# Moving whole rounds of a short convolution from TensorE to VectorE, in front of a chain of matrix products

## The chip, the cores and the metric

One NeuronCore of a Trainium2 chip runs the kernel. TensorE multiplies matrices into PSUM, VectorE (DVE) and ScalarE (ACT) evict and combine, GpSimd (POOL) casts while it starts DMAs, SyncE (SP) starts the other DMAs and the transposing ones. The metric is the device time of one execution in microseconds (us), the median over runs; before the change it is 519.52 (519.33 to 520.88, three runs).

## The reference

The input x has 8 sequences of 3904 tokens with 192 channels. First comes a causal convolution of 7 taps along the tokens; the taps of each of the 8 heads (24 channels each) are a softmax. Its output goes, token by token, through two products side by side, their elementwise product, and two further products:

```
w   = softmax(weight)                            # 8 heads x 7 taps
out[b, s, c] = sum_k w[head(c), k] * x_padded[b, s + k, c]
a = out @ w1; b = out @ w2                       # 192 -> 1024
h = a * b @ w3                                   # 1024 -> 1024
result = h @ w_out                               # 1024 -> 192
```

The kernel multiplies w3 by w_out once at its start (`w3_product`, into W_sb), so that two products are left per token: the first (192 to 2 x 1024) and the second (1024 to 192).

## The kernel before

**Tokens.** The 31232 tokens are two streams (r = 0, 1) of 15616. A round R is 512 tokens of both streams; there are 31, the last one half as long. `first_product(R)` makes, for each of eight slices ft of 128 columns, the halves pa and pb: six matmuls each of 64 rows x 512 columns (three channel groups, two streams), the two streams on the two halves of the array's rows. ScalarE casts pa to asb (line 464), VectorE multiplies asb by pb into abT (line 466). pa, pb and all other PSUM tiles share four buffers of two banks (`banks`). `second_product(R, r)` multiplies abT by W_sb into ops (line 482), ScalarE copies it to osb (line 487), SP stores it (line 490).

**Phases.** After a start in which rounds 0 to 2 have their first product between all the loading of weights, the loop runs phases p = 0 to 14. Phase 0 has no first product; phase p has those of rounds 2p+1 and 2p+2. Then come the second products of rounds 2p and 2p+1, four in all. Every engine executes its instructions in the order in which the program gives them; nothing reorders them. SP and POOL are such queues too: a DMA that must wait holds back all DMAs that are behind it on its engine. SP's DMAs use eight completion semaphores in turn, so that each also waits for the landing of the one eight places ahead.

**The convolution on TensorE.** Windows of 32 tokens (26 new ones and 6 of overlap) are loaded by POOL into xb and cast to bf16 (`load_x`, line 127). A unit (`conv`) multiplies the windows of one block, for some heads' channels, by 32x32 banded matrices of the taps (line 296, into cps); ScalarE evicts to convo (line 305). When a block is complete, `store` writes it by SP to the DRAM tensor rows (lines 331, 337), and `transposes(R)` reads 512 tokens back with a transposing DMA for each of three groups k of 64 channels (both streams side by side, 128 rows) into the ring xT, which has place for four rounds (line 371). The first product reads xT. Blocks 0 to 3 have 20, 20, 20 and 40 windows and all 192 channels; blocks 4 to 11 have 64 (the last 56) and only the first 128 channels. Units of 48 and of 64 matmuls alternate; the table `places` puts one or two of them into a phase, behind its first and its third second product.

**The convolution on VectorE.** From round 5 on, the last 64 channels (k = 2) are VectorE's. `cast_c` copies two rounds of x by POOL to the DRAM tensor rows_c in bf16 (line 396), `raw_transpose` brings them by one transposing DMA of 1040 columns to the tile raw (line 402), and `conv_c` applies the seven taps with a multiplication and multiply-adds over 1024 columns (lines 412, 416), the last of them into xT[2]. The taps come as a column per channel, wC: SP stores the softmax to DRAM and reads it back spread over the partitions (`load_taps`, lines 379, 385). The call of `conv_c` in phase p stands between the first products and the second products, for the rounds of phase p+1; the raw transpose for the next phase is issued at a phase's end, ahead of the xT transposes.

**Loads.** From phase 1 on, POOL issues one block of x a phase, after a tiny copy (`pace`) that waits for the last multiply of the phase's first round.

## Time and profile before

| what | value |
|---|---|
| median of three runs | 519.52 us |
| the profiled execution's own time | 521.78 us |
| its span, first to last instruction | 519.8 us |
| TensorE busy | 512.5 us, 99% |
| VectorE busy | 423.0 us, 81% |
| ScalarE busy | 339.0 us, 65% |
| POOL busy | 82.3 us, 16% |
| mean granted clock of TensorE | 0.997 |
| first product, one matmul of 64x512 | 373 ns, two at a time |
| multiply into abT | 1221 ns, 240 of them |

The chain of work that ended last is 96% TensorE's. A group's idle time is the time of its engine just before it, with what ended most of it. In the chain in order of time and in the timeline, the first number is the start in us from the span's start, the second the length. In the table of windows the columns are the length, then each engine's busy time with its number of instructions (PE, PEld, DVE, ACT, POOL), the granted clock of TensorE, the busy share of the DMA engines and GB/s. SPq marks SP's issuing of DMAs.

### The profile page before, as it was taken

Reading aid. Unit: us, or ns where it says so; the run is one execution under the profiler, and the core shown is the slowest. Engines: PE = TensorE matmul, PEld = TensorE weight load, DVE = VectorE, ACT = ScalarE, POOL = GpSimd, SP = SyncE. Lnnn points to the kernel's source line nnn. Section 1 sums busy time; section 2 is a strip of 40 time slices with the busy share of each in tenths; the row PEclk is TensorE's granted clock in tenths of the full one; section 3 lists DMA queues with packets and bytes.
Section 4 is the critical chain, followed back from the end, with each engine's and each line's share of the span. In section 5 each row is a group of like instructions: output and inputs, shape, how many; then the busy total and the mean of one; then the engine's idle time right before and its main releaser. Section 6 shows DMA issues by size and latency. Waiting matters only on the chain.

```text
span 519.8 us, 14514 instructions
## 1 busy us (share of the span) xinstructions
PE 512.5 (99%) x6276; PEld 337.7 (65%) x6276; DVE 423.0 (81%) x408; ACT 339.0 (65%) x368; POOL 82.3 (16%) x143
## 2 busy tenths in 40 slices
PE   8999999899999999999999999999999999999997
PEld 4446846647658475584755858558485584856777
DVE  6898187599797996979979799797997979979670
ACT  6886586476675757757566575767757657476562
POOL 8866003023030220302700000000000000000000
PEclk9999999899999999999999999999999999999999
DMA  9999979969597697955991422905615076240304
GB/s 139 152 182 147 151 167 148 189 123 126 154 95 144 135 127 156 144 129 82 176 214 32 132 53 58 183 12 128 122 60 126 1 181 62 63 106 3 122 1 153
DMA packets 164270, 60.76 MB, mean 117 GB/s; under 512 B 113139, under 2 KB 164207, under 8 KB 164207
## 3 DMA queue, kind: packets, MB, share of 16 engines
q1 hardware_dynamic: 92719, 42.65, 36.7%
q0 software_dynamic: 71472, 17.19, 36.2%
q8 instruction: 49, 0.80, 0.6%
q14 instruction: 14, 0.11, 0.1%
q10 hardware_dynamic: 16, 0.00, 0.0%
HBM read 34.66 MB, written 34.82 MB: 134 GB/s over the span
## 4 chain that ended last, share of the span: by engine, by line
PE 96%; ACT 1%; DMA 1%; issue 1%; DVE 1%; POOL 0%; DVEq 0%; POOLq 0%
PE ops L482 32%; PE pa L457 30%; PE pb L457 30%; PE cps L296 2%; PE wps L547 1%; DMA xb<-in_x_dram 1%; ACT asb L464 1%; DVE abT L466 0%; ACT convo L305 0%; PE ops L500 0%; PE tps L361 0%; PE tps L346 0%; POOL xb L127 0%; DVE xT L353 0%; PE warm L206 0%
## 5 line engine op out<-in xcount | busy, mean ns | idle before, releaser
L466 DVE TENSOR_TENSOR abT<-asb,pb 128x1024 bf16<-128x1024 bf16 x240 | 292.9, 1221 | 72.5 <-ACT asb L464 56.8
L464 ACT CAST asb<-pa 128x1024 bf16<-128x1024 f32 x244 | 247.0, 1012 | 63.4 <-PE pa L457 63.1
L457 PE MATMUL pb<-xT,wn 64*128 64x512 bf16 (+1 forms) x744 | 198.3, 373 | 0.0
L457 PE MATMUL pa<-xT,wn 64*128 64x512 bf16 (+1 forms) x744 | 197.5, 373 | 0.2
L457 PE MATMUL pa<-xT,ws 64*128 64x512 bf16 (+1 forms) x744 | 197.5, 373 | 0.0
L457 PE MATMUL pb<-xT,ws 64*128 64x512 bf16 (+1 forms) x744 | 196.2, 373 | 0.0
L457 PEld LDWEIGHTS <-wn 64*128 64x128 bf16 x1488 | 138.2, 94 | 86.0 <-issue 2.2
L457 PEld LDWEIGHTS <-ws 64*128 64x128 bf16 x1488 | 131.8, 94 | 70.8 <-POOL ws L192 0.4
L482 PE MATMUL ops<-W_sb,abT 128*128 128x192 bf16 x1936 | 166.8, 247 | 0.0
L482 PEld LDWEIGHTS <-abT 128*128 128x128 bf16 x1936 | 159.6, 98 | 7.2 <-issue 6.2
L487 ACT COPY osb<-ops 128x768 f32<-128x768 f32 (+1 forms) x61 | 48.4, 794 | 102.9 <-PE ops L482 102.9
L416 DVE SCALAR_TENSOR_TENSOR acc<-raw,wC,acc 128x1024 f32<-128x1024 bf16 (+8 forms) x80 | 83.0, 1066 | 1.9
L305 ACT CAST convo<-cps 128x1024 bf16<-128x1024 f32 (+3 forms) x46 | 37.7, 876 | 3.9 <-PE cps L296 3.8
L127 POOL DMA_DIRECT2D xb<-in_x_dram x54 | 38.0, 713 | 2.8 <-PE pa L457 1.6
L638 POOL COPY pace<-abT 1x2 bf16<-1x2 bf16 x6 | 1.0, 174 | 161.3 <-DVE abT L466 161.3
L396 POOL DMA_DIRECT2D rows_c<-in_x_dram x26 | 19.8, 766 | 3.5 <-issue 2.4
L416 DVE SCALAR_TENSOR_TENSOR xT<-raw,wC,acc 128x512 bf16<-128x512 bf16 (+1 forms) x26 | 18.1, 739 | 0.4
L296 PE MATMUL cps<-xb,Aband 32*32 32x192 bf16 (+6 forms) x1216 | 14.6, 225 | 2.5 <-issue 2.0
L296 PEld LDWEIGHTS <-Aband 32*32 32x32 bf16 x1216 | 10.6, 88 | 8.2 <-issue 7.0
L412 DVE TENSOR_SCALAR acc<-raw,wC 128x1024 f32<-128x1024 bf16 (+1 forms) x13 | 9.7, 749 | 2.1 <-DMA raw<-rows_c 2.1
L504 DVE COPY osb<-ops 128x192 f32<-128x192 f32 x1 | 0.4, 358 | 11.7 <-PE ops L500 11.7
L528 POOL DMA_DIRECT2D w3b<-in_moe_w_dram x12 | 7.1, 598 | 4.0 <-DMA xb<-in_x_dram 3.4
(63 smaller groups left out, 75.0 us busy)
## 6 DMA issues: line engine op xcount, KB each, us to landing
out_dram<-osb SPq DMA_DIRECT2D x60, 384.0 KB
xb<-in_x_dram POOLq DMA_DIRECT2D x16, 256.0 KB, 7.0
rows<-convo SPq DMA_DIRECT2D x25, 128.0 KB
rows_c<-in_x_dram POOLq DMA_DIRECT2D x22, 128.0 KB, 5.8
rows<-convo SPq DMA_DIRECT2D x25, 80.0 KB
xb<-in_x_dram POOLq DMA_DIRECT2D x8, 240.0 KB, 6.8
xb<-in_x_dram POOLq DMA_DIRECT2D x6, 216.0 KB, 5.5
w3b<-in_moe_w_dram POOLq DMA_DIRECT2D x4, 256.0 KB, 5.0
```

What stands on the lines that cost most here:

```text
L127: nc.gpsimd.dma_start(out=xb[group(r, e), s:s + w, :], in_=bass.AP(tensor=x.tensor, offset=(r * TS + t - PAD) * D, ap=[[D, C], [E * ST * D ...
L296: nc.tensor.matmul(o.rearrange("p (w g) -> p w g", g=wd)[:, :, c - c0:c1 - c0], Aband[group(r, e), h, :], xb[group(r, e), s:s + m, c:c1], ...
L305: f(out=convo[:, e::E, k, :, lo:lo + c] .rearrange("p w r g -> p r w g"), in_=src[:, :, :, o:o + c])
L396: nc.gpsimd.dma_start(out=rows_c[t0:t1, r * Q:r * Q + Q], in_=x_rows[r * TS + t0:r * TS + t1, WC:D])
L412: nc.vector.tensor_scalar(out=out, in0=raw[:, HALO + lo - t0 - d:HALO + hi - t0 - d], scalar1=wC[:, K - 1 - d:K - d], scalar2=None, op0=AL ...
L416: nc.vector.scalar_tensor_tensor(out=out, in0=raw[:, HALO + lo - t0 - d:HALO + hi - t0 - d], scalar=wC[:, K - 1 - d:K - d], in1=acc[:, lo ...
L457: nc.tensor.matmul(p[:, r, f * N:f * N + N], w_of(i, k, r)[rs, ft * 128:(ft + 1) * 128], xT[k][rs, r0:r0 + N], start=(k == 0), stop=(k == ...
L464: nc.scalar.copy(out=asb[:, :, 0:per * N], in_=pa[:, :, 0:per * N])
L466: nc.vector.tensor_tensor(out=ab[:, f0, :, 0:N], in0=asb[:, :, 0:N], in1=pb[:, :, 0:N], op=ALU.mult)
L482: nc.tensor.matmul(ops[:, g // 2, (g % 2) * D:(g % 2) * D + D], ab[:, jt, r, g * 128:(g + 1) * 128], W_sb[:, jt, :], start=(jt == 0), stop ...
L487: nc.scalar.copy(out=osb.rearrange("p (a g) d -> p a (g d)", g=2), in_=ops[:, 0:ng // 2, 0:2 * D])
L528: nc.gpsimd.dma_start(out=t[C * i:C * i + C], in_=bass.AP(tensor=moe_w3.tensor, offset=j0 * 128 * DFF + i * GQ, ap=[[DFF, C], [C * DFF, 4 ...
```

## The change

The four phases 4, 7, 10 and 13 (SIDE) get the convolution of both their rounds, all three channel groups, from VectorE; all other rounds get it from TensorE.

- `side_cast`, `side_transpose` and `side_conv` take the place of `cast_c`, `raw_transpose` and `conv_c`: one channel group k of one SIDE phase at a time. Phases 1, 2, 3 convolve k = 0, 1, 2 for phase 4, phases 4, 5, 6 for phase 7, and so on to phase 12. The result is the tile side, which the first product reads in place of xT (`operand`). Input, accumulator and result live in buffers that the loading of w3 used. The raw transpose is two DMAs (528 and 512 columns).
- TensorE's blocks have all 192 channels: sizes 40, 40, 80, 80, 80 and 32 after block 3. Blocks 6, 7 and 8 (80 windows) feed the four rounds between two SIDE phases. Units have two heads (32 matmuls, 240 columns) in the blocks of 80 and four heads (64 matmuls) in the others. Block 6 is stored in phase 3, block 7 in phase 6, block 8 in phase 9, and their twelve transposes are issued at that phase's end, for the phase after next.
- At a phase's end the xT transposes are issued first and the raw ones behind them.
- `load_taps` moves from the loads of round 0's first product to the end of round 2's, behind the transposes of rounds 3 and 4; it fills 64 partitions for all three groups with ten DMAs, and POOL copies them to the other 64 at the start of phase 1.
- Loads of x and casts are lists of single DMAs (`x_jobs`), of which some are issued after each of five slices of a phase's first products, each time behind a `pace` copy.
- In phase 0 the two units stand behind the first and the second of the second products, and VectorE evicts half of each.
- The outputs of the last two rounds are stored in halves, and the last two copies change engines.

```diff
-    SIZES = [20, 20, 20, 40] + [64] * 7 + [56]
-    SPLIT = 4
+    SIDE = (4, 7, 10, 13)
+    SIZES = [20, 20, 20, 40, 40, 40, 80, 80, 80, 32]
...
+    def side_transpose(p, k):
+        t0, t1 = side_span(p)
+        raw_of[p, k] = stage.tile([128, HALO + 2 * CH], BF16, tag="w3T", bufs=2, name="raw")
+        for lo, hi in ((t0 - HALO, t0 + CH), (t0 + CH, t1)):
+            nc.sync.dma_start_transpose(
+                out=raw_of[p, k][:, HALO + lo - t0:HALO + hi - t0], in_=rows_c[lo:hi, k, :])
+
+    def side_conv(p, k):
+        t0, t1 = side_span(p)
+        if p not in side_of:
+            side_of[p] = stage.tile([128, NP, 2 * CH], BF16, tag="w3b0", bufs=1, name="side")
+        raw = raw_of.pop((p, k))
+        acc = stage.tile([128, 2 * CH], FP32, tag="w3b4", bufs=1, name="acc")
...
+        for d in range(2, K):
+            for lo, hi in zip([t0] + [z + d for z in starts], starts + [t1]):
+                add(acc[:, lo - t0:hi - t0], lo, hi, d)
+        add(side_of[p][:, k, :], t0, t1, 0)
+
+    def operand(R, k, rs):
+        if phase_of(R) in SIDE:
+            t0 = R * CH - side_span(phase_of(R))[0]
+            return side_of[phase_of(R)][rs, k, t0:t0 + width(R)]
+        a = ring_of[R] * CH % RING
+        return xT[k][rs, a:a + width(R)]
...
-        load_taps()
-        cast_c(0)
+        for f in side_cast(SIDE[0], 0):
+            f()
         load_x(5)
...
-               (store, 3), (transposes, 3), (transposes, 4))})
+               (store, 3), (transposes, 3), (transposes, 4), (load_taps,))})
...
-    places = {0: 2, 1: 2, 2: 1, 3: 1, 4: 2, 5: 1, 6: 1, 7: 1, 8: 1, 9: 2, 10: 1, 11: 1}
+    places = {0: (0, 1), 1: (0, 2), 2: (0, 2), 3: (0, 2), 4: (0,), 5: (0,), 6: (0, 2), 7: (0,),
+              8: (0,), 9: (0, 2), 10: (0,), 11: (0,)}
+    tasks = {q - NP + k: (q, k) for q in SIDE for k in range(NP)}
+    jobs = {p: side_cast(*tasks[p + 1]) for p in range(1, len(phases)) if p + 1 in tasks}
+    for p, b, part in ((1, 6, 0), (1, 6, 1), (2, 7, 0), (3, 7, 1), (5, 8, 0), (6, 8, 1), (8, 9, 0)):
+        jobs[p] = jobs.get(p, []) + x_jobs(b, part)
+    points = ((0, 1), (0, 4), (0, 7), (1, 2), (1, 5))
...
+        if p == 1:
+            P(out=wC[Q:128], in_=wC[0:Q])
...
-        if 0 < p <= len(chunks):
-            conv_c(p - 1)
+        if p in tasks:
+            side_conv(*tasks[p])
...
-        if p < len(chunks):
-            raw_transpose(p)
-        while sent[0] < NR and sent[0] <= LAG + 2 * p + 4 and \
-                min((sent[0] + 1) * CH, TS) <= stored[0]:
-            transposes(sent[0])
-            sent[0] += 1
+        while due:
+            transposes(due.pop(0))
+        if p + 1 in tasks:
+            side_transpose(*tasks[p + 1])
```

More of the change, by code (lines that the diff above doesn't have):

```diff
@@ L46, with phase_of, windows @@
     ST = C - PAD
-    WB = -(-S // ST)
-    NWIN = (B // NS) * WB
-    LAST = S - (WB - 1) * ST
     LAG_ROWS = (LAG + 1) * CH
-    SIZES = [20, 20, 20, 40] + [64] * 7 + [56]
-    SPLIT = 4
-    WC = 2 * Q
-    assert sum(SIZES) == NWIN
+    SIDE = (4, 7, 10, 13)
+    SIZES = [20, 20, 20, 40, 40, 40, 80, 80, 80, 32]
     NB = len(SIZES)
     FIRST = [sum(SIZES[:b]) for b in range(NB)]
-    RC = FIRST[SPLIT] * ST // CH
-    XN = 32 * WC
+    XN = 20 * D
     HW = 6
+    def phase_of(R):
+        return (R - 1) // 2
+    def windows(t0, t1):
+        out = []
+        while t0 < t1:
+            n = min(ST, t1 - t0, S - t0 % S)
+            a = min(t0, TS - ST)
+            out.append((a, t0 - a, t0 - a + n))
+            t0 += n
+        return out
+    conv_rounds = [R for R in range(NR) if phase_of(R) not in SIDE]
+    ring_of = {R: i for i, R in enumerate(conv_rounds)}
+    t0 = (LAG + 3) * CH
+    spans = [(0, t0), (t0, t0 + SIZES[4] * ST), (t0 + SIZES[4] * ST, (2 * SIDE[0] + 1) * CH)]
+    for q, nxt in zip(SIDE, SIDE[1:] + (NR,)):
+        spans.append(((2 * q + 3) * CH, min((2 * nxt + 1) * CH, TS)))
+    wins = []
+    for i, (t0, t1) in enumerate(spans):
+        ws = windows(t0, t1)
+        size = sum(SIZES[:4]) if i == 0 else SIZES[3 + i]
+        assert len(ws) <= size
+        wins += ws + [(ws[-1][0], 0, 0)] * (size - len(ws))
+    assert len(wins) == sum(SIZES)
     def tok(i):
-        return (i // WB) * S + (i % WB) * ST
+        return wins[i][0]
     const = ctx.enter_context(tc.tile_pool(name="const", bufs=1))
@@ L80 @@
     rows = dram.tile([TS, NP * NS * Q], BF16, name="rows")
-    rows_c = dram.tile([TS, NS * Q], BF16, name="rows_c")
+    rows_c = dram.tile([TS, NP, NS * Q], BF16, name="rows_c")
     taps_d = dram.tile([H, K], FP32, name="taps_d")
@@ L89, in shape_of @@
         return n, m, n // m
-    def width_of(b):
-        return D if b < SPLIT else WC
     def parts_of(b):
-        return [range(4)] if 4 * shape_of(b)[1] * width_of(b) <= XN else [range(2), range(2, 4)]
+        return [range(4)] if 4 * shape_of(b)[1] * D <= XN else [range(2), range(2, 4)]
     xb_of, zero_rows = {}, {}
@@ L105, in runs_of @@
         for s, i in enumerate(FIRST[b] + j * n + u * E + e for j in js for u in range(m)):
-            if i < HW or i == NWIN - 1:
+            if i < HW:
                 continue
@@ L112, in runs_of, with x_jobs, alloc @@
         return runs
-    def load_x(b, parts=(0, 1)):
+    def x_jobs(b, part):
+        js = parts_of(b)[part]
+        n, m, E = shape_of(b)
         tiles = xb_of.setdefault(b, {})
-        zeros_of = zero_rows.setdefault(b, [])
-        n, m, E = shape_of(b)
-        for js in [v for q, v in enumerate(parts_of(b)) if q in parts]:
-            wd = width_of(b)
+        def alloc():
             xb = work.tile([128, XN], BF16, tag="xb", bufs=6, name="xb")
-            xb = xb[:, 0:len(js) * m * wd].rearrange("p (w d) -> p w d", d=wd)
+            xb = xb[:, 0:len(js) * m * D].rearrange("p (w d) -> p w d", d=D)
@@ L122, in load_x @@
             for j in js:
                 tiles[j] = (xb, (j - js[0]) * m)
-            for e in range(E):
-                for s, t, w in runs_of(b, js, e):
-                    for r in range(NS):
-                        nc.gpsimd.dma_start(
-                            out=xb[group(r, e), s:s + w, :],
-                            in_=bass.AP(tensor=x.tensor, offset=(r * TS + t - PAD) * D,
-                                        ap=[[D, C], [E * ST * D, w], [1, wd]]))
-                for j in js:
-                    for u in range(m):
-                        i, s = FIRST[b] + j * n + u * E + e, tiles[j][1] + u
-                        if i % WB == 0 and i:
-                            zeros_of += [(xb, group(r, e).start, s) for r in range(NS)]
-                        if i == NWIN - 1:
-                            nc.gpsimd.memset(xb[group(1, e), s, :], 0.0)
-                            t = tok(i) - PAD
-                            nc.gpsimd.dma_start(out=xb[group(0, e), s, :],
-                                                in_=x_rows[t:t + C, 0:wd])
-                            p = group(1, e).start
-                            nc.gpsimd.dma_start(out=xb[p:p + PAD + LAST, s, :],
-                                                in_=x_rows[TS + t:TS + t + PAD + LAST, 0:wd])
@@ new lines, in alloc, with job, run @@
+                for e in range(E):
+                    for u in range(m):
+                        i = FIRST[b] + j * n + u * E + e
+                        if tok(i) % S == 0 and i:
+                            zero_rows.setdefault(b, []).extend(
+                                (xb, group(r, e).start, tiles[j][1] + u) for r in range(NS))
+        def job(first, r, e, s, t, w):
+            def run():
+                if first:
+                    alloc()
+                nc.gpsimd.dma_start(
+                    out=tiles[js[0]][0][group(r, e), s:s + w, :],
+                    in_=bass.AP(tensor=x.tensor, offset=(r * TS + t - PAD) * D,
+                                ap=[[D, C], [E * ST * D, w], [1, D]]))
+            return run
@@ L146, with load_x @@
+        todo = [(r, e, s, t, w) for e in range(E) for s, t, w in runs_of(b, js, e)
+                for r in range(NS)]
+        return [job(i == 0, *a) for i, a in enumerate(todo)]
+    def load_x(b):
+        for part in range(len(parts_of(b))):
+            for f in x_jobs(b, part):
+                f()
     taps = const.tile([H, K], FP32)
@@ L281, in conv @@
         if b not in convo_of:
-            convo_of[b] = work.tile([128, n, width_of(b) // Q, NS, Q], BF16, tag="convo", bufs=2,
+            convo_of[b] = work.tile([128, n, NP, NS, Q], BF16, tag="convo", bufs=2,
                                     name="convo")
-            left_of[b] = width_of(b) * E
+            left_of[b] = D * E
         convo = convo_of[b]
@@ L310, in conv @@
             del xb_of[b]
-    stored, sent = [0], [3]
     def store(b, first=0):
-        stored[0] = tok(FIRST[b] + SIZES[b]) if b + 1 < NB else TS
         n = SIZES[b] // 4
         convo = convo_of[b]
-        cols = slice(0, NS * width_of(b))
         for j in range(4):
@@ L321, in store @@
             while w < n:
-                i = FIRST[b] + j * n + w
+                i, m = FIRST[b] + j * n + w, 1
+                t, s0, s1 = wins[i]
+                while w + m < n and wins[i + m] == (t + m * ST, 0, ST):
+                    m += 1
                 if i < first:
-                    w += 1
-                    continue
-                left = WB - 1 - i % WB
-                src = convo[C * j:C * j + ST, w:w + max(1, min(n - w, left))]
-                src = src.rearrange("s w k r g -> s w (k r g)")
-                j0 = tok(i)
-                if left == 0:
-                    nc.sync.dma_start(out=rows[j0:j0 + LAST, cols], in_=src[0:LAST, 0, :])
-                    w += 1
-                    continue
-                m = min(n - w, left)
-                dst = rows[j0:j0 + ST * m, cols].rearrange("(w s) c -> s w c", s=ST)
-                for s0, s1 in ((0, 16), (16, ST)):
-                    nc.sync.dma_start(out=dst[s0:s1], in_=src[s0:s1])
+                    m = first - i
+                elif s1 - s0 < ST:
+                    m = 1
+                    if s1:
+                        nc.sync.dma_start(
+                            out=rows[t + s0:t + s1, :],
+                            in_=convo[C * j + s0:C * j + s1, w].rearrange("s k r g -> s (k r g)"))
+                else:
+                    src = convo[C * j:C * j + ST, w:w + m].rearrange("s w k r g -> s w (k r g)")
+                    dst = rows[t:t + ST * m, :].rearrange("(w s) c -> s w c", s=ST)
+                    for s0, s1 in ((0, 16), (16, ST)):
+                        nc.sync.dma_start(out=dst[s0:s1], in_=src[s0:s1])
                 w += m
@@ L368, in transposes @@
         t0, t1 = max(R * CH, first), min((R + 1) * CH, TS)
-        a = t0 % RING
-        for k in range(NP if R < RC else WC // Q):
+        a = ring_of[R] * CH % RING + t0 - R * CH
+        for k in range(NP):
             nc.sync.dma_start_transpose(
@@ L375 @@
     HALO = 16
-    wC = const.tile([128, K], FP32)
+    wC = const.tile([128, NP, K], FP32)
     def load_taps():
         nc.sync.dma_start(out=taps_d, in_=taps)
-        for r in range(NS):
-            c = WC
-            while c < D:
-                h = c // G
-                c1 = min(h * G + G, D)
-                nc.sync.dma_start(out=wC[r * Q + c - WC:r * Q + c1 - WC, :],
-                                  in_=taps_d[h:h + 1, :].to_broadcast([c1 - c, K]))
-                c = c1
-    chunks = [(R * CH, min((R + 2) * CH, TS)) for R in range(RC, NR, 2)]
@@ L390 @@
-    raw_of = {}
-    def cast_c(i):
-        t0, t1 = chunks[i]
-        t0 = t0 if i else t0 - HALO
-        for r in range(NS):
-            nc.gpsimd.dma_start(out=rows_c[t0:t1, r * Q:r * Q + Q],
-                                in_=x_rows[r * TS + t0:r * TS + t1, WC:D])
-    def raw_transpose(i):
-        t0, t1 = chunks[i]
-        raw_of[i] = work.tile([128, HALO + 2 * CH], BF16, tag="raw", bufs=2, name="raw")
-        nc.sync.dma_start_transpose(out=raw_of[i][:, 0:HALO + t1 - t0],
-                                    in_=rows_c[t0 - HALO:t1, :])
@@ L405, in conv_c @@
-    def conv_c(i):
-        t0, t1 = chunks[i]
-        raw = raw_of.pop(i)
-        acc = work.tile([128, 2 * CH], FP32, tag="acc", bufs=1, name="acc")
-        starts = [z for z in range(0, TS, S) if t0 <= z < t1]
-        def times(out, lo, hi, d):
-            nc.vector.tensor_scalar(out=out, in0=raw[:, HALO + lo - t0 - d:HALO + hi - t0 - d],
-                scalar1=wC[:, K - 1 - d:K - d], scalar2=None, op0=ALU.mult)
+        c = 0
+        while c < D:
+            h = c // G
+            c1 = min(h * G + G, (c // Q + 1) * Q)
+            nc.sync.dma_start(out=wC[c % Q:c % Q + c1 - c, c // Q, :],
+                              in_=taps_d[h:h + 1, :].to_broadcast([c1 - c, K]))
+            c = c1
@@ new lines, with side_span, side_cast, job @@
+    raw_of, side_of = {}, {}
+    def side_span(p):
+        return (2 * p + 1) * CH, (2 * p + 3) * CH
+    def side_cast(p, k):
+        t0, t1 = side_span(p)
+        def job(r):
+            def run():
+                nc.gpsimd.dma_start(
+                    out=rows_c[t0 - HALO:t1, k, r * Q:r * Q + Q],
+                    in_=x_rows[r * TS + t0 - HALO:r * TS + t1, k * Q:k * Q + Q])
+            return run
+        return [job(r) for r in range(NS)]
+    def side_transpose(p, k):
[4 more added lines that the diff above has]
+                out=raw_of[p, k][:, HALO + lo - t0:HALO + hi - t0], in_=rows_c[lo:hi, k, :])
@@ new lines, in side_conv @@
+    def side_conv(p, k):
+        t0, t1 = side_span(p)
+        if p not in side_of:
+            side_of[p] = stage.tile([128, NP, 2 * CH], BF16, tag="w3b0", bufs=1, name="side")
+        raw = raw_of.pop((p, k))
+        acc = stage.tile([128, 2 * CH], FP32, tag="w3b4", bufs=1, name="acc")
+        starts = [z for z in range(0, TS, S) if t0 <= z < t1]
+        nc.vector.tensor_scalar(
+            out=acc, in0=raw[:, HALO - 1:HALO - 1 + t1 - t0], scalar1=wC[:, k, K - 2:K - 1],
+            scalar2=None, op0=ALU.mult)
+        for z in starts:
+            nc.vector.memset(acc[:, z - t0:z - t0 + 1], 0.0)
@@ L417, in add @@
                 out=out, in0=raw[:, HALO + lo - t0 - d:HALO + hi - t0 - d],
-                scalar=wC[:, K - 1 - d:K - d], in1=acc[:, lo - t0:hi - t0],
+                scalar=wC[:, k, K - 1 - d:K - d], in1=acc[:, lo - t0:hi - t0],
                 op0=ALU.mult, op1=ALU.add)
-        times(acc[:, 0:t1 - t0], t0, t1, 1)
-        for z in starts:
-            nc.vector.memset(acc[:, z - t0:z - t0 + 1], 0.0)
         for d in range(2, K):
@@ L426, in conv_c @@
                 add(acc[:, lo - t0:hi - t0], lo, hi, d)
-        for lo in range(t0, t1, CH):
-            hi = min(lo + CH, t1)
-            add(xT[2][:, lo % RING:lo % RING + hi - lo], lo, hi, 0)
+        add(side_of[p][:, k, :], t0, t1, 0)
[5 more added lines that the diff above has]
+        return xT[k][rs, a:a + width(R)]
     def w_of(i, k, r):
@@ L444, in first_product @@
         abT_of[R] = ab
-        r0 = (R * CH) % RING
         per = CH // N if CH % N == 0 else 1
@@ L459, in first_product @@
                                 w_of(i, k, r)[rs, ft * 128:(ft + 1) * 128],
-                                xT[k][rs, r0:r0 + N],
+                                operand(R, k, rs),
                                 start=(k == 0), stop=(k == NP - 1))
@@ L488, in second_product @@
                        in_=ops[:, 0:ng // 2, 0:2 * D])
-        t0 = r * TS + R * CH
-        nc.sync.dma_start(
-            out=out[t0:t0 + ng * 128, :].rearrange("(g p) d -> p g d", p=128), in_=osb)
+        n = ng if R < NR - 2 else ng // 2
+        for g in range(0, ng, n):
+            t0 = r * TS + R * CH + g * 128
+            nc.sync.dma_start(
+                out=out[t0:t0 + n * 128, :].rearrange("(g p) d -> p g d", p=128),
+                in_=osb[:, g:g + n, :])
         if r == 1:
@@ L496, in last_product @@
         ab = abT_of.pop(R)
-        for g, f in zip(range(width(R) // 128), (nc.scalar.copy, nc.vector.tensor_copy) * 2):
+        for g, f in zip(range(width(R) // 128), (nc.vector.tensor_copy, nc.scalar.copy) * 2):
             ops = banks("ops")
@@ L588, in later_loads @@
         nc.gpsimd.tensor_scalar(out=taps, in0=taps, scalar1=total, scalar2=None, op0=ALU.mult)
-        load_taps()
-        cast_c(0)
+        for f in side_cast(SIDE[0], 0):
+            f()
         load_x(5)
@@ L608, with convolve @@
                (conv, 3, 96, 96, (A,), (0,)), (conv, 3, 96, 96, (V,), (1,)),
-               (store, 3), (transposes, 3), (transposes, 4))})
-    sent[0] = 5
+               (store, 3), (transposes, 3), (transposes, 4), (load_taps,))})
     phases = [()] + [(R, R + 1) for R in range(LAG + 1, NR, 2)]
     assert phases[-1][-1] == NR - 1
-    units = [(b, c) for b in range(SPLIT, NB) for c in range(0, WC, Q)]
-    loads = [(b, e) for b in range(6, NB) for e in range(len(parts_of(b)))]
-    def convolve():
-        b, c = units.pop(0)
-        conv(b, c, Q, (A, A))
-        if c + Q == WC:
+    units = [(b, h, n) for b in range(4, NB)
+             for n in [max(v for v in (2, 4) if v * shape_of(b)[1] * G <= CH)]
+             for h in range(0, H, n)]
+    places = {0: (0, 1), 1: (0, 2), 2: (0, 2), 3: (0, 2), 4: (0,), 5: (0,), 6: (0, 2), 7: (0,),
+              8: (0,), 9: (0, 2), 10: (0,), 11: (0,)}
+    assert sum(map(len, places.values())) == len(units)
+    tasks = {q - NP + k: (q, k) for q in SIDE for k in range(NP)}
[3 more added lines that the diff above has]
+    points = ((0, 1), (0, 4), (0, 7), (1, 2), (1, 5))
+    sent = [LAG + 3]
+    due = []
+    def convolve(p):
+        b, h, n = units.pop(0)
+        conv(b, h * G, n * G, (V, A) if p not in tasks else (A, A))
+        if h + n == H:
             store(b)
-    places = {0: 2, 1: 2, 2: 1, 3: 1, 4: 2, 5: 1, 6: 1, 7: 1, 8: 1, 9: 2, 10: 1, 11: 1}
-    assert sum(places.values()) == len(units)
+            while sent[0] < len(conv_rounds) and \
+                    min((conv_rounds[sent[0]] + 1) * CH, TS) <= spans[b - 3][1]:
+                due.append(conv_rounds[sent[0]])
+                sent[0] += 1
     pace = const.tile([1, 2], BF16)
@@ L628, with issue, run @@
     for p, rounds in enumerate(phases):
-        for b, c in units[:2]:
+        for b in {u[0] for u in units[:3]}:
             for xb, p0, w in zero_rows.pop(b, []):
                 nc.gpsimd.memset(xb[p0:p0 + PAD, w, :], 0.0)
-        if 0 < p < len(chunks):
-            cast_c(p)
-        for j, R in enumerate(rounds):
-            first_product(R)
-            if loads and j == 0:
-                nb, part = loads.pop(0)
-                P(out=pace, in_=abT_of[R][0:1, JT - 1, 1, 0:2])
-                load_x(nb, (part,))
-        if 0 < p <= len(chunks):
-            conv_c(p - 1)
+        if p == 1:
+            P(out=wC[Q:128], in_=wC[0:Q])
+        todo = jobs.pop(p, [])
+        def issue(R, ft, n):
+            def run():
+                P(out=pace, in_=abT_of[R][0:1, ft, 1, 0:2])
+                for _ in range(min(n, len(todo))):
+                    todo.pop(0)()
+            return run
+        each = -(-len(todo) // len(points))
+        for j, R in enumerate(rounds):
+            first_product(R, {ft: issue(R, ft, each) for a, ft in points if a == j and todo})
+        assert not todo
+        if p in tasks:
+            side_conv(*tasks[p])
         last = NR if p == len(phases) - 1 else done + 2
@@ L646 @@
             (last_product if (R, r) == (NR - 1, NS - 1) else second_product)(R, r)
-            if n in (0, 2)[:places.get(p, 0)]:
-                convolve()
-        if p < len(chunks):
-            raw_transpose(p)
-        while sent[0] < NR and sent[0] <= LAG + 2 * p + 4 and \
-                min((sent[0] + 1) * CH, TS) <= stored[0]:
-            transposes(sent[0])
-            sent[0] += 1
-    assert not units and not loads
-    assert done == NR and sent[0] == NR
+            if n in places.get(p, ()):
+                convolve(p)
+        while due:
+            transposes(due.pop(0))
+        if p + 1 in tasks:
+            side_transpose(*tasks[p + 1])
+    assert not units and not due and not jobs and done == NR and sent[0] == len(conv_rounds)
 _INS = ['x', 'weight', 'moe_w1', 'moe_w2', 'moe_w3', 'moe_w_out']
```

## The prediction

> **What bounds the kernel now.** I read the page's busy line and its chain first.

> ```profile
> PE 512.5 (99%) x6276; PEld 337.7 (65%) x6276; DVE 423.0 (81%) x408; ACT 339.0 (65%) x368; POOL 82.3 (16%) x143
> ...
> PE 96%; ACT 1%; DMA 1%; issue 1%; DVE 1%; POOL 0%; DVEq 0%; POOLq 0%
> ```

> TensorE bounds it, and the other engines matter only where they make TensorE wait. The chain in order of time shows a clean stretch and the one bad place.

> ```profile
> 94.20 0.54 PE cps L296 x50
> 94.74 1.96 issue
> 96.70 0.22 PE cps L296 x8
> 96.92 4.40 PE ops L482 x32
> 101.32 0.75 PE pa L457 x6
> ...
> 445.32 10.67 PE ops L482 x128
> 455.99 0.75 PE pa L457 x6
> ...
> 476.81 10.67 PE ops L482 x128
> ```

> A phase is two rounds of first product (476.81 - 455.99 = 20.82 us) and four second products (10.67), 31.49 together. Phases with one convolution unit begin 32.15 apart (133.48 to 165.69 is 32.21), so 48 matmuls cost 0.67; with two, 32.87 (165.69 to 198.56), so the 64-matmul unit costs 0.71. Phase 1 has two units and takes 36.6: TensorE idles 1.96 and then needs 4.40 for 32 matmuls that take 2.75 elsewhere, 1.65 more. The windows say why:

> ```profile
> 93.98:97.39 3.41, 1.46 (x74) 1.14 (x72) 3.33 (x4) 1.22 (x2) 0.00 (x0) 1.00 1.56 245
> 97.39:100.81 3.42, 3.42 (x24) 3.25 (x22) 0.66 (x1) 1.51 (x2) 0.00 (x0) 0.50 0.75 192
> ```

> After the stretch with 1.96 us of idling the granted clock is 0.50 for 3.42 us. One short stall thus cost 3.6.

> Next, VectorE and SP in the same phase: the side convolution is VectorE's, and its input comes through SP's queue.

> ```profile
> 89.24 0.75 DVE L412 TENSOR_SCALAR acc<-raw,wC 128x1024 f32<-128x1024 bf16 x1 [2.07 <-DMA raw<-rows_c]
> 90.03 6.57 DVE L416 SCALAR_TENSOR_TENSOR acc<-raw,wC,acc 128x1024 f32<-128x1024 bf16 x5
> 96.63 1.42 DVE L416 SCALAR_TENSOR_TENSOR xT<-raw,wC,acc 128x512 bf16<-128x512 bf16 x2
> ```

> ```profile
> 40.29 0.29 SPq L379 DMA_DIRECT2D taps_d<-taps  x1
> 44.78 3.27 SPq L385 DMA_DIRECT2D wC<-taps_d  x6
> ...
> 57.71 8.94 SPq L371 DMA_TRANSPOSE xT<-rows  x6
> 66.69 2.01 SPq L490 DMA_DIRECT2D out_dram<-osb  x3
> 68.81 7.34 SPq L337 DMA_DIRECT2D rows<-convo  x8
> ...
> 78.04 2.35 SPq L402 DMA_TRANSPOSE raw<-rows_c  x1
> 80.48 8.59 SPq L371 DMA_TRANSPOSE xT<-rows  x4
> ...
> 359.49 5.52 SPq L337 DMA_DIRECT2D rows<-convo  x8
> ...
> 365.97 2.05 SPq L402 DMA_TRANSPOSE raw<-rows_c  x1
> 368.11 5.12 SPq L371 DMA_TRANSPOSE xT<-rows  x4
> ```

> The raw transpose is issued at 78.04, ahead of the four xT transposes, and even so VectorE gets it at 89.2 and waits 2.07. It finishes at 98.05, 3.3 us before the next phase: TensorE does not notice. That slack is the cover that the change uses up.

> **The change, part by part.**

> *SP's queue in phases 0 and 1.* The load of the taps moves from ahead of the first row stores (SP sat there idle until 40.29, harmless) to behind the transposes of rounds 3 and 4, and it grows from 6 to 10 DMAs. Behind it now queue the outputs of phase 0, block 4's stores, six transposes (were four) and last the two raw transposes that the side convolution of phase 1 reads. I add up when they land:
> - Transposes end at 66.65; the stores ahead of them no longer wait for the taps (the waits list 1.8 us there): 65.5.
> - taps_d 0.3, then its landing: 44.78 - 40.58 = 4.2. At 70.0.
> - Ten wC at 3.27 / 6 = 0.55: 75.5.
> - Two outputs at 2.01 / 3 = 0.67, eight stores at 7.34 / 8 = 0.92, two outputs: 85.5.
> - Six transposes: between 5.12 / 4 = 1.28 (late row) and 8.59 / 4 = 2.15 (this stretch); I take the middle, 1.72, since POOL's loads overlap only part of it: 95.8. Two raw halves the same: 99.2.
> - Landing after issue: round 3's last transpose is issued at about 62.4 and its product starts unhindered at 64.69, so at most 2.3; the raw one above took 89.2 - 80.4 = 8.8 with POOL's loads in flight. I take 4: 103.2. Ends: 95 (stores at 0.69 as in the 359.49 row, transposes at 1.28, landing 2) and 111.5.

> VectorE executes in order: it waits in the side convolution until 103.2, needs 0.75 + 6.57 + 1.42 = 8.8, and only then reaches the first multiply of phase 2 (1221 ns): 113.2. TensorE, if it had no stall of its own, would begin phase 2 at 64.7 + 20.82 + 10.67 + 2 x 0.74 = 97.7 and can run five half-products of 0.65 before the sixth needs the PSUM buffer that this multiply frees: 100.9. It waits 12.3. Before, it reached the same point at 101.32 + 3.25 = 104.6, so the net is +8.6, and +1.65 for the clock after the stall. The old 1.96 us stall, should it stay, lies inside this wait. Bounds: 0 to +17.

> *The same queue after each block of 80.* Blocks 6, 7 and 8 are stored at the end of phases 3, 6 and 9, followed by twelve transposes and then the two raw ones for phases 4, 7 and 10. With T the start of those phases' first product: stores begin at T - 0.7 (359.49 against 360.16). Nine stores; the rows of eight with 64 windows cost 0.69 each, 80 windows 0.86: T + 7.0. Output 0.7, twelve transposes at 1.30 with their gaps 15.6, two raw 2.6: T + 25.9; landing 2 (POOL has only two casts there): T + 27.9. Convolution 8.8 and multiply 1.2: T + 37.9. TensorE needs it at 10.67 + 20.82 + 0.6 + 3.25: T + 35.35. A stall of 2.6, three times. Bounds 0 (stores at 0.6, landing 1.5) and 5 (transposes at 1.5, landing 2.5). Before, raw went first and VectorE never waited after phase 1.

> The clock after such a short stall: the row above has half clock after 1.96 us of idling, worth 1.65; a stall split over two stretches may escape, so I take half, 0.8. Three times 3.4 is +10.2. [...]

> *TensorE's convolution.* Sixteen units of 48 and 64 matmuls after block 3 (8 x 1.38 = 11.0) become six of 64 (0.74, between the 0.71 above and the 0.77 of a unit of block 3, at 43.17, with what it adds to the product behind it) and twelve of 32. None of 32 is in the trace: 16 more matmuls cost 0.04 to 0.05, so 0.61; bounds 0.35 (in proportion) and 0.77. 4.4 + 7.3 = 11.7: +0.8, between -2.4 and +2.7.

> *Costed at nothing.* VectorE has 12 side convolutions instead of 13, in TensorE's shadow. ScalarE's evictions come in two pieces (700 + 434 against 1025 ns), about 0.2 a unit, beside 10 us idle a phase. POOL copies wC at the start of phase 1 and so waits for it until about 79: nine of phase 1's twelve paced loads and casts then leave in a heap; the loads are due only in phase 2's second half, but they meet SP's transposes (counted in the landing). In later phases pacing hides behind first products. The split outputs of the last rounds end where they did: the last copy was 0.36 and becomes 0.32.

> **Sum.** 8.6 + 1.65 + 10.2 + 0.8 = +21.3 on the profiled execution's 521.78 (span 519.8): 543. That execution stands 2.26 above the median of the runs; taken off, 541.

> **Rivals.**
> 1. *Only phase 1 stalls.* The later stalls are small differences of long sums, and without POOL's loads SP may issue stores faster. For it: the 5.52 row; against: 14 transposes cannot be issued under 18 us. +10.3 + 0.8: 530.6.
> 2. *Only the blocks of 80 stall*, raw lands in time in phase 1, and with it TensorE's 3.6 goes, since fewer matmuls and smaller loads surround it. -3.6 + 10.2 + 0.8: 527.
> 3. *Faster.* The x loads carry the same bytes in fewer, wider rows (192 instead of 128 columns), the transfers of phase 1 thin out, raw lands before 90.9 there and before T + 25.3 later, and all that is left is the 3.6 us hole, gone: 521.78 - 3.6 + 0.8 - 2.26 = 516.7. For it: DMA share 1.56 in the stretch of the hole. Against: even without contention the sum gives 95.
> 4. *Worse.* Transfers pile up: raw at 111.5 (+16.9), stalls of 5, each with half clock: 559.

> **How the numbers follow.** Forecast 0.48 (its own range 529 to 553); rival 1 0.20; rival 2 0.08; rival 3 0.12; rival 4 0.06; parts that cancel to within 0.3% (1.6 us, what a measurement here can tell) 0.06. Faster is rival 3, same the cancelling, slower the rest, 0.82. The range 519 to 553 leaves out rival 3 and rival 4.

> **What would show it.** VectorE's first side operation of phase 1 waits for raw from about 86 to 103, and TensorE idles at about 101 for some 12 us with VectorE's multiply as the releaser; the same with 2 to 3 us at the starts of phases 5, 8 and 11, and none at 3, 4, 6. SP's row has raw behind six and twelve transposes. If VectorE's waits are there but TensorE has no hole, the slack was larger than I read; if raw lands before 91, the queue's steps are shorter than their rows.

## The result and the profile after

The changed kernel takes 563.5 us (560.9 to 565.91) against 519.52 us (519.25 to 521.6): 1.0834 times the kernel before, 95% interval 1.0789 to 1.0878. That is 44 us slower where 21 were forecast, and outside the range of 519 to 553. The profiled execution took 564.64 us with a span of 562.9.

TensorE's busy time and the chain, from the page of the changed kernel:

```profile
PE 520.9 (93%) x6148; PEld 339.8 (60%) x6148; DVE 417.2 (74%) x410; ACT 340.4 (60%) x392; POOL 88.1 (16%) x180
...
PE 83%; DVE 6%; DMA 5%; SPq 2%; issue 2%; ACT 1%; POOL 1%; DVEq 0%; POOLq 0%; ACTq 0%
```

VectorE and the DMAs now stand in the chain with 6% and 5%, 11% of 562.9 or some 62 us together; TensorE's share fell from 96% to 83%. The waits of the changed kernel (total, times, longest) say where:

```profile
DVE acc L437 <- DMA raw<-rows_c: 54.1, 4, 16.5
...
PE pb L486 <- DVE abT L495: 23.7, 3, 8.7
...
PE pa L486 <- DVE abT L495: 8.2, 1, 8.2
...
PE cps L318 <- issue: 3.1, 1, 3.1
```

VectorE waits four times for raw, 54.1 us in all, and four times TensorE then waits for VectorE's multiply: 23.7 + 8.2 = 31.9 us. The first wait for raw stands in phase 1 and holds TensorE up at the start of phase 2; by VectorE's timeline and SP's:

```profile
104.32 0.75 DVE L437 TENSOR_SCALAR acc<-raw,wC 128x1024 f32<-128x1024 bf16 x1 [16.53 <-DMA raw<-rows_c]
105.11 6.57 DVE L444 SCALAR_TENSOR_TENSOR acc<-raw,wC,acc 128x1024 f32<-128x1024 bf16 x5
111.71 1.28 DVE L444 SCALAR_TENSOR_TENSOR side<-raw,wC,acc 128x1024 bf16<-128x1024 bf16 x1
112.91 2.35 DVE L495 TENSOR_TENSOR abT<-asb,pb 128x1024 bf16<-128x1024 bf16 x2
```

```profile
63.83 1.37 SPq L398 DMA_DIRECT2D taps_d<-taps  x1
66.52 3.71 SPq L403 DMA_DIRECT2D wC<-taps_d  x10
70.33 0.97 SPq L521 DMA_DIRECT2D out_dram<-osb  x2
71.41 7.41 SPq L356 DMA_DIRECT2D rows<-convo  x8
78.91 1.61 SPq L521 DMA_DIRECT2D out_dram<-osb  x2
83.69 13.74 SPq L390 DMA_TRANSPOSE xT<-rows  x6
97.55 2.89 SPq L427 DMA_TRANSPOSE raw<-rows_c  x2
...
178.11 10.54 SPq L356 DMA_DIRECT2D rows<-convo  x8
188.70 1.41 SPq L349 DMA_DIRECT2D rows<-convo  x1
190.20 1.00 SPq L521 DMA_DIRECT2D out_dram<-osb  x1
191.30 17.58 SPq L390 DMA_TRANSPOSE xT<-rows  x12
209.05 2.45 SPq L427 DMA_TRANSPOSE raw<-rows_c  x2
```

The queue is the one foreseen: the taps, the outputs, the stores, the xT transposes, and raw last. The lower half is the end of phase 3 (the next phase's first product starts at 178.62), and the same pattern stands at 285.43 and 392.76. There VectorE gets raw at 213.1, 34.5 us after that start, and its multiply for phase 5 begins at 221.84. In the chain the hole of TensorE and what follows it:

```profile
221.84 1.22 DVE abT L495
...
223.10 1.46 PE pb L486 x6
224.57 1.28 PE pa L486 x6
225.85 1.28 PE pb L486 x6
227.13 1.28 PE pa L486 x6
```

Six matmuls that take 0.65 take 1.28 after the hole: half clock. The windows of 3.41 us:

```profile
215.43:218.84 3.41, 0.42 (x4) 0.09 (x1) 3.41 (x6) 0.00 (x0) 0.00 (x0) 1.00 0.95 262
218.84:222.25 3.41, 0.00 (x0) 0.00 (x0) 3.38 (x5) 0.00 (x0) 0.00 (x0) 0.50 0.13 28
222.25:225.67 3.42, 2.57 (x14) 1.12 (x15) 3.42 (x4) 1.01 (x1) 0.94 (x2) 0.50 0.00 0
225.67:229.08 3.41, 3.41 (x20) 1.39 (x18) 2.00 (x2) 1.65 (x2) 0.94 (x2) 0.50 1.19 76
229.08:232.50 3.42, 3.42 (x34) 1.74 (x32) 2.47 (x3) 2.40 (x3) 1.38 (x2) 1.00 0.65 63
```

The sum of the loss, from the gaps between TensorE's instructions and the clock's windows:

| place | idle, us | work done at half clock, us | its loss |
|---|---|---|---|
| start of phase 2 | 7.7 | 5.7 | 2.8 |
| start of phase 5 | 7.7 | 6.0 | 3.0 |
| start of phase 8 | 9.2 | 3.0 | 1.5 |
| start of phase 11 | 8.2 | 3.0 | 1.5 |
| phase 1, second unit, against before | +1.1 | | +0.1 |

The four holes come to 32.8 us, their half clock to 8.8 and phase 1 to 1.2: 42.8, near the 43.1 by which the span grew. That it fits so well is in part chance, since small terms outside the table cancel: by their lengths the four phases are 42.4 us longer than the same phases of the version called both below (the table has 41.6 for them), phase 1 begins 0.6 later, and TensorE's convolution is 1.2 shorter from phase 2 on. Undisturbed phases with as many units are no longer than before (within 0.1 us): a phase with two units of 32 matmuls takes 32.42 (146.20 to 178.62) where one with 48 and 64 took 32.87.

### The profile page after: what moved, and what is told of

Read it like the earlier page. It is cut to its first block, busy times and chain, and to the rows that moved or that the text cites. A ratio compares the mean times of both kernels' runs of the same rounds, so it can differ in the third digit from the quotient of the medians.

```text
span 562.9 us, 14352 instructions
## 1 busy us (share of the span) xinstructions
PE 520.9 (93%) x6148; PEld 339.8 (60%) x6148; DVE 417.2 (74%) x410; ACT 340.4 (60%) x392; POOL 88.1 (16%) x180
## 4 chain that ended last, share of the span: by engine, by line
PE 83%; DVE 6%; DMA 5%; SPq 2%; issue 2%; ACT 1%; POOL 1%; DVEq 0%; POOLq 0%; ACTq 0%
PE ops L511 27%; PE pb L486 27%; PE pa L486 26%; DVE acc L444 4%; DMA raw<-rows_c 3%; PE cps L318 2%; DMA xb<-in_x_dram 1%; DVE abT L495 1%; PE wps L579 1%; SPq L427 1%; SPq L390 1%; DMA wn<-in_moe_w_dram 1%; DVE acc L437 1%; ACT asb L493 0%; POOL xb L152 0%
## 5 line engine op out<-in xcount | busy, mean ns | idle before, releaser
L495 DVE TENSOR_TENSOR abT<-asb,pb 128x1024 bf16<-128x1024 bf16 x240 | 292.0, 1221 | 66.5 <-ACT asb L493 49.2
L486 PE MATMUL pb<-xT,wn 64*128 64x512 bf16 (+1 forms) x552 | 151.8, 381 | 23.7 <-DVE abT L495 23.7
L486 PE MATMUL pa<-xT,wn 64*128 64x512 bf16 (+1 forms) x552 | 150.0, 380 | 9.3 <-DVE abT L495 8.2
L486 PE MATMUL pa<-xT,ws 64*128 64x512 bf16 (+1 forms) x552 | 150.1, 381 | 0.0
L486 PE MATMUL pb<-xT,ws 64*128 64x512 bf16 (+1 forms) x552 | 148.9, 382 | 0.0
L444 DVE SCALAR_TENSOR_TENSOR acc<-raw,wC,acc 128x1024 f32<-128x1024 bf16 (+10 forms) x90 | 78.7, 925 | 1.3
L486 PE MATMUL pb<-side,wn 64*128 64x512 bf16 x192 | 52.0, 376 | 0.0
L486 PE MATMUL pa<-side,wn 64*128 64x512 bf16 x192 | 51.8, 376 | 0.0
L486 PE MATMUL pa<-side,ws 64*128 64x512 bf16 x192 | 51.7, 376 | 0.0
L486 PE MATMUL pb<-side,ws 64*128 64x512 bf16 x192 | 51.4, 376 | 0.0
L437 DVE TENSOR_SCALAR acc<-raw,wC 128x1024 f32<-128x1024 bf16 x12 | 9.0, 750 | 54.1 <-DMA raw<-rows_c 54.1
L327 ACT CAST convo<-cps 128x640 bf16<-128x640 f32 (+4 forms) x70 | 39.1, 635 | 5.5 <-PE cps L318 5.4
```

Of the source, the lines that this page charges most:

```text
L327: f(out=convo[:, e::E, k, :, lo:lo + c] .rearrange("p w r g -> p r w g"), in_=src[:, :, :, o:o + c])
L437: nc.vector.tensor_scalar(out=acc, in0=raw[:, HALO - 1:HALO - 1 + t1 - t0], scalar1=wC[:, k, K - 2:K - 1], scalar2=None, op0=ALU.mult)
L444: nc.vector.scalar_tensor_tensor(out=out, in0=raw[:, HALO + lo - t0 - d:HALO + hi - t0 - d], scalar=wC[:, k, K - 1 - d:K - d], in1=acc[:, ...
L486: nc.tensor.matmul(p[:, r, f * N:f * N + N], w_of(i, k, r)[rs, ft * 128:(ft + 1) * 128], operand(R, k, rs), start=(k == 0), stop=(k == NP ...
L495: nc.vector.tensor_tensor(out=ab[:, f0, :, 0:N], in0=asb[:, :, 0:N], in1=pb[:, :, 0:N], op=ALU.mult)
```

## The experiments

Theory A: raw's place in SP's queue makes the holes. Theory B, the rival: the DMA engines are overloaded where a block of 80 is stored, and the order only decides who is late.

**Raw first.** At a phase's end only these lines change places:

```diff
-        while due:
-            transposes(due.pop(0))
         if p + 1 in tasks:
             side_transpose(*tasks[p + 1])
+        while due:
+            transposes(due.pop(0))
```

> The changed kernel with the two raw transposes issued ahead of the xT transposes at each phase's end; nothing else is different. Theory A (the place in SP's queue makes the stalls): in phases 4, 7 and 10 raw lands about 17 us after the phase's start, VectorE reaches its side convolution later than that and does not wait, and the holes of 7.3, 8.8 and 8.2 us at the starts of phases 5, 8 and 11 go with their stretches of half clock, -31 us. In phase 1 raw lands near 95 instead of 104, which is in time for the product's block at 106.5: another 7.7 and 2.8. Time about 522, at most 532 if phase 1 stays late. Theory B (the DMA engines are overloaded where a block of 80 is stored, whatever the order): the lateness only moves to the xT transposes, TensorE waits for xT at the starts of phases 2, 5, 8 and 11 instead, and the time stays above 545.

Measured: 523.94 us (520.64 to 526.08), 1.0074 of the kernel before (1.0048 to 1.0101). The exchange gives back 39.6 of the 44 us. The waits for raw fall from four to one:

```profile
DVE acc L437 <- DMA raw<-rows_c: 10.3, 1, 10.3
...
PE cps L318 <- issue: 2.8, 1, 2.8
...
PE pa L486 <- DMA xT<-rows: 0.8, 1, 0.8
PE pb L486 <- DVE abT L495: 0.8, 1, 0.8
```

The holes at phases 5, 8 and 11 are gone and nothing stands in their place: the twelve xT transposes, now later by the two raw ones, still land before they are read. In phase 1 VectorE got raw at 97.45, not at 95, and its multiply still held TensorE up by 0.8 us at the start of phase 2. Only there did a small part of the lateness move to xT, another 0.8 us. Theory B is out for the later phases.

**The taps early, raw still last.** `load_taps` goes back to its old place, ahead of the first stores:

```diff
         nc.gpsimd.tensor_scalar(out=taps, in0=taps, scalar1=total, scalar2=None, op0=ALU.mult)
+        load_taps()
         for f in side_cast(SIDE[0], 0):
...
-               (store, 3), (transposes, 3), (transposes, 4), (load_taps,))})
+               (store, 3), (transposes, 3), (transposes, 4))})
```

> The changed kernel with the load of the taps where the kernel before has it, ahead of the first stores of rows; the raw transposes stay behind the xT transposes. Theory A: SP reaches phase 0's outputs 6.4 us earlier (63.8 instead of 70.3), raw lands near 98, and the hole of 7.7 us at the start of phase 2 shrinks to 1 to 2 us with less half clock; the three later holes stay as they are. Time 553 to 557. Theory B: the transfers of phase 1 are bound by the DMA engines, the earlier start is eaten up, and the time stays within 3 us of 563.5.

Measured: 558.11 us (557.45 to 559.52), 1.074 (1.0687 to 1.0793), 5.4 faster than the change: between the two expectations, a little nearer to theory A's. VectorE's timeline of this run:

```profile
99.66 0.75 DVE L437 TENSOR_SCALAR acc<-raw,wC 128x1024 f32<-128x1024 bf16 x1 [12.41 <-DMA raw<-rows_c]
...
108.26 2.35 DVE L495 TENSOR_TENSOR abT<-asb,pb 128x1024 bf16<-128x1024 bf16 x2
```

SP issued raw 7.6 us earlier (90.0 instead of 97.55), VectorE got it 4.7 earlier. The other 2.9 went into a slower issue (3.63 instead of 2.89 for the two) and a longer landing. TensorE too came earlier to the start of phase 2, since its hole in phase 1 was 1.5 instead of 3.1, with no half clock behind it; so the wait there fell only from 7.7 to 6.8 and not to 1 or 2. In phase 1 theory B has a share: part of an earlier issue is eaten up.

**Both.**

> Both: raw ahead of xT and the taps loaded early. Theory A: no wait of VectorE for raw over 1 us and no hole of TensorE but the one in phase 1's second unit (3.1 us, then half clock for 3.4). By the phases' lengths (a unit of 32 matmuls costs 0.47, so that TensorE's convolution is 1.2 shorter than before, and that hole is 1.1 longer) the time is that of the kernel before within 2 us: 518 to 522. Theory B: above 540.

Measured: 518.23 us (517.3 to 519.28), 0.9959 (0.9935 to 0.9983). All that the change lost is back, and a little more. VectorE still waits 2.8 us for raw in phase 1, where under 1 was expected, but TensorE does not notice. TensorE's waits are the start's and one other:

```profile
PE cps L318 <- issue: 1.2, 1, 1.2
PE warm L228 <- DVE zeros L172: 1.1, 1, 1.1
```

The hole in phase 1 is 1.2 us, shorter than in any version so far, and the clock stays at 1.00 after it. Against the kernel before that is 0.8 + 1.65, and the cheaper convolution about 1.2.

**The order alone, in the kernel before.** Its raw transpose moves behind its four xT transposes.

> The kernel before with its raw transpose moved behind the four xT transposes of each phase. Theory A: in phase 1 raw lands near 97 instead of 89.2, VectorE ends at about 106 and TensorE is held up for 1 to 3 us at the start of phase 2, with up to 1.7 for the clock; later phases do not notice, because four transposes take 5.2 us and VectorE reaches the side convolution some 10 us after that. Time 520 to 524. Theory B: no difference, 519.5.

Measured: 528.56 us (525.1 to 529.71), 1.0152 (1.0099 to 1.0205): slower by 8.3, twice what was expected at most, though the interval leaves open whether it is over 2%. The direction is theory A's. The profiled execution was the fastest of the four, 525.1, and shows the expected place:

```profile
96.87 0.75 DVE L412 TENSOR_SCALAR acc<-raw,wC 128x1024 f32<-128x1024 bf16 x1 [9.62 <-DMA out_dram<-osb]
97.66 6.57 DVE L416 SCALAR_TENSOR_TENSOR acc<-raw,wC,acc 128x1024 f32<-128x1024 bf16 x5
104.26 1.42 DVE L416 SCALAR_TENSOR_TENSOR xT<-raw,wC,acc 128x512 bf16<-128x512 bf16 x2
```

VectorE starts at 96.87 instead of 89.24 (the profile puts the wait down to an output's landing, but VectorE waits here for several semaphores, raw's among them, and the operands are raw's). It writes xT[2] until 105.7, and the first product of phase 2 reads that: TensorE waits 2.96 for it. I had put the wait one multiply later. Why the other executions took 3 to 4.6 more is open; they have a lower mean clock (0.994 in the one of 528.26, 0.990 in the other two), but there is no trace of them.

**The dose.** The version of both, but where twelve transposes follow a block, raw stands behind nine:

```diff
+        if len(due) == 4:
+            for R in due[:3]:
+                transposes(R)
+            del due[:3]
         if p + 1 in tasks:
             side_transpose(*tasks[p + 1])
```

> The version with raw first and the taps early, but where twelve transposes follow a block of 80 (ends of phases 3, 6, 9) the raw ones stand behind nine of them. Theory A, by dose: three transposes are three times 1.47 = 4.4 us (17.58 for 12), so that raw lands 4.4 earlier than in the changed kernel and the holes at the starts of phases 5, 8 and 11 are 7.3, 8.8 and 8.2 less 4.4: 2.9, 4.4 and 3.8 us. Each should leave a window of 3.41 us with under half of it busy, and be followed by one or two windows of half clock (1.5 to 3 us each). 518.2 + 11 + 4.5 to 9: 534 to 538. Theory B: the holes do not follow the number of transposes ahead.

Measured: 536.64 us (535.29 to 538.37), 1.03 (1.0274 to 1.0325); the holes are 4.4, 4.4 and 3.7 us, and the windows of half clock two, two and one. The line of the waits (total, times, longest):

```profile
PE pa L486 <- DVE abT L495: 12.4, 3, 4.4
```

The two windows at the first of these holes, in columns as above:

```profile
200.07:203.48 3.41, 0.00 (x0) 0.00 (x0) 3.37 (x5) 0.34 (x1) 0.00 (x0) 1.00 0.98 298
203.48:206.90 3.42, 2.52 (x13) 1.01 (x14) 3.10 (x3) 1.01 (x1) 0.94 (x2) 0.50 0.35 79
```

With none, nine and twelve transposes ahead the holes are 0, about 4.2 and about 8.4: beyond the slack, each of the last three transposes costs TensorE 1.4 us, which is what one of the nine took (12.73 together), and the clock adds to it.

**The hole in phase 1.** It is called "issue": TensorE waits for nothing that the profile shows, in the middle of a unit of short matmuls, in a stretch where the busy share of the DMA engines is 1.56 in the kernel before (93.98 to 97.39) and 1.57 in the changed one (94.50 to 97.90). To see whether the transfers cause it, x loads were taken out of phase 1, in the version of both (block 6 in phase 2, block 7 in phase 3) and in the kernel before:

```diff
-    for p, b, part in ((1, 6, 0), (1, 6, 1), (2, 7, 0), (3, 7, 1), (5, 8, 0), (6, 8, 1), (8, 9, 0)):
+    for p, b, part in ((2, 6, 0), (2, 6, 1), (3, 7, 0), (3, 7, 1), (5, 8, 0), (6, 8, 1), (8, 9, 0)):
```

> The version with raw first and the taps early, and the x loads of block 6 issued in phase 2 instead of phase 1, those of block 7 in phase 3. Theory: the hole of 1.2 to 3.1 us (the profile's issue) in the second convolution unit of phase 1 is an instruction fetch of TensorE that is late because POOL's and SP's transfers fill the DMA engines there; with ten loads fewer in phase 1 it is under 0.5 us, and the time 1 to 1.5 below 518.2: about 517. Rival: the hole belongs to the unit's dense instructions alone and stays at 1 us or more.

Measured: 527.28 us (525.99 to 528.04), 1.0126 (1.0105 to 1.0146). The hole is gone, as the theory has it, but the forecast time was wrong, since the loads came too late for phase 2's first unit:

```profile
PE cps L318 <- DMA xb<-in_x_dram: 6.1, 4, 3.2
```

Ten loads, handed out by their pacing from 104.2 to 116.1, are waited for from 121.5 to 128.5 (the one that TensorE waits for last lands 14.1 us after its issue), and half clock follows. The kernel before has longer until it needs the block:

```diff
-            if loads and j == 0:
+            if loads and j == 0 and p > 1:
```

> The kernel before, with its x loads starting in phase 2 instead of phase 1 (each block one phase later). The same two theories for its own hole of 1.96 us and the 1.65 of half clock behind it: with the transfers as cause both go, 519.5 - 3.6 = about 516; as a matter of instructions alone they stay, 519.5.

Measured: 518.13 us (517.69 to 520.11), 0.9958 (0.9938 to 0.9978), 2.8 below the median of the kernel before and not 3.6. The profiled execution's span is 516.1 instead of 519.8, the 3.6 of the hole and its half clock; but not every execution of the kernel before loses the clock (three of the ten measured beside this run have a mean clock of 0.997, the others 0.999 or 1.000).

```profile
88.76 5.39 PE ops L482 x64
94.15 0.61 PE cps L296 x58
94.75 2.75 PE ops L482 x32
97.50 0.75 PE pa L457 x6
```

No hole at 94.75, and the 32 matmuls behind it take 2.75 instead of 4.40. So the hole needs POOL's loads in phase 1; the rival, dense instructions alone, is out.

The traces speak for the loads delaying TensorE's instructions. The profile lists a queue "q8 instruction", the row behind the fetch of the expectations, with 49 transfers in the kernel before (0.80 MB) and 48 in the changed one (0.79 MB), of 16384 bytes each. TensorE has 2 x 6276 and 2 x 6148 matmuls and weight loads there, 256 for each transfer in both, so I take the queue for TensorE's. In all seven profiles that have the hole, of both kernels, TensorE stops behind the same 1372nd matmul, and it goes on 1.3 to 1.7 us after the queue's tenth transfer has ended. TensorE's own columns up to the end of the hole, in the kernel before and in the changed one:

```profile
0.00:96.69 96.69, 92.74 (x1372) 57.43 (x1373) 70.89 (x88) 66.42 (x83) 44.72 (x83) 1.00 1.27 158
0.00:98.20 98.20, 92.28 (x1372) 57.18 (x1372) 66.43 (x85) 64.70 (x85) 47.73 (x94) 1.00 1.16 151
```

The tenth transfer ran from 93.9 to 95.2 in the kernel before (hole until 96.70) and from 95.3 to 96.8 in the changed one (until 98.23). In the versions without x loads in phase 1 it began at 89.2 and 89.3, and there is no hole. No run shows what holds this transfer back, and that TensorE waits for it is read from these times alone.

**A version below both.** Both, with half of block 6's loads left in phase 1:

```diff
-    for p, b, part in ((1, 6, 0), (1, 6, 1), (2, 7, 0), (3, 7, 1), (5, 8, 0), (6, 8, 1), (8, 9, 0)):
+    for p, b, part in ((1, 6, 0), (2, 6, 1), (3, 7, 0), (3, 7, 1), (5, 8, 0), (6, 8, 1), (8, 9, 0)):
```

> The version with raw first and the taps early; of block 6 the first half of x is loaded in phase 1, as in the change, and the second half in phase 2 (block 7 in phase 3). Theory: half the loads leave TensorE's instruction fetch in phase 1 enough of the DMA engines, so that the hole of 1.2 us is under 0.5, and five loads early in phase 2 land before the unit at 121.5 that waited 6.1 us in all where ten did. Then the time is 517 or a little less, and below both kernels. If the second half still lands late, a wait for xb of 1 to 3 us stands at 121.5 and the time is 518 to 521.

Measured: 516.84 us (516.61 to 517.3), 0.9942 (0.9924 to 0.9961), the lowest median of all, though this interval overlaps those of 0.9959 and 0.9958 above. The queue's tenth transfer begins at 91.2 here, and there is no hole. After the start, TensorE has no wait over 0.3 us:

```profile
PE warm L228 <- DVE zeros L172: 1.1, 1, 1.1
PE cps L318 <- DMA xb<-in_x_dram: 0.4, 2, 0.3
```

## Why the prediction was right in kind and wrong in size

The step that failed is the price of SP's queue after a block of 80, and with it the length of the three later stalls. The sum was 21.8 us short (21.3 against 43.1), and 21.6 of that stand here: the three stalls with their clock were to cost 10.2 and cost 31.8 by the lengths of phases 5, 8 and 11.

- **SP's queue in phases 0 and 1: right, in its time partly by luck.** Raw was to land at 103.2 and the multiply to end at 113.2; VectorE started at 104.32 and the multiply ended at 114.14. The single terms were less good: the taps landed after 1.3 us instead of 4.2 and the ten wC took 3.71 instead of 5.5, so SP was through with the outputs at 80.5 and not at 85.5; then it waited 3.1 for the stores to land, which the sum did not have, and the six transposes took 13.74 instead of 10.3. These cancelled. TensorE's wait of 12.3 came as 3.1 in the unit, with half clock, and 7.7 at the phase's start. That the old stall would lie inside the wait was right. (The lower end of 95 for raw should have been 96 by its own terms.)
- **The queue after a block of 80: the mechanism was right, the three places too, and this term was mis-sized.** It had raw land 27.9 us after the phase's start; VectorE got it at 34.5. "80 windows 0.86" scaled the row of 0.69 for 64 windows by the number of windows alone. But the rows had become 384 columns wide instead of 256: 5.52 x 1.25 x 1.5 = 10.35, and the eight stores took 10.54. With the ninth, 11.95 stands against 7.7. The last block's eight stores bear this out: 32 windows took 3.96 us (at 461.30), where bytes give 5.52 x 0.5 x 1.5 = 4.1 and windows alone 2.8. The twelve transposes took 17.58 instead of 15.6. In the prediction's sum the slack was used up already, so these microseconds went into the hole: 7.7, 9.2 and 8.2 instead of 2.6. (For raw at 34.5 the prediction's own sum gives 9.2; at phase 5 TensorE got through seven half-products of 0.65 before it waited, not five, and so lost 7.7.)
- **The clock: the row was the right guide, and its half weight was the mistake.** 0.8 for each later stall became 1.5 to 3.0, since each of the stalls (7.7, 9.2 and 8.2 us) held a window with 0.00 us busy, and the granted clock was 0.50 for 10.24, 10.24 and 6.83 us, of which TensorE works through 6.0, 3.0 and 3.0.
- **TensorE's units.** Twelve of 32 matmuls cost 0.47 each (32.42 less 31.49, halved) instead of 0.61, near the lower bound; the convolution was 1.2 cheaper than before, not 0.8 dearer.
- **The range** took the later stalls at 5 us at most. With 1.5 for the width in the stores' price each would have been 3.9 longer, and the upper end of 553 some 12 higher, about 565 by this estimate: it would have held the time.
- **The rivals.** The only one on the other side needed raw before 90.9 in phase 1, and both kinds of stall came, so the first three rivals are out. The fourth, at 559, is nearest in time: raw was not as late in phase 1 as it asked, but its stalls of 5 us with half clock at each came, and longer.

## What to carry to other kernels

Before adding work to a queue, list what stands behind it and read off for each the latest time that its reader can bear; here two transposes with some 3 us of slack were put behind twelve of which the first has about 10 and the last six a phase more, and exchanging them gave back 39.6 of 44 us. When a row's duration is scaled to a new shape, scale it by bytes as well as by count: the eight stores took 10.54 us where both give 10.35 and the count alone 6.9. And a hole in the engine that bounds the kernel can cost more than its length: the 7.7 us at phase 5 cost 3.0 more at a granted clock of 0.50.

## What the runs showed that I had not expected

- **How short an idle time takes the clock.** The windows of granted clock are 3.41 us long. After a window with 1.46 us busy the next had 0.50 (the kernel before), and after 0.42 or 0.00 too. The closest pair is 1.51 us busy with 0.50 after it (raw first, the first row) and 1.59 with 1.00 after it (the order alone, the other two):

```profile
95.41:98.82 3.41, 1.51 (x53) 1.41 (x54) 1.33 (x2) 0.95 (x3) 0.00 (x0) 1.00 1.48 135
100.51:103.92 3.41, 1.59 (x17) 1.03 (x15) 3.34 (x3) 0.80 (x1) 0.00 (x0) 1.00 0.86 135
103.92:107.34 3.42, 2.27 (x22) 1.25 (x23) 2.52 (x4) 1.56 (x2) 0.00 (x0) 1.00 0.85 176
```
